# Attention block on one core: SyncE's wait for the output stores moved behind the closing barrier, its first loads moved ahead of the block

## Chip, cores, metric

One core of one Trainium2 chip. The metric is the device time of one execution in microseconds (us); each kernel is run several times, and where two kernels are compared they ran in turns on the same chip. A run more than 1.5% above the fastest of its kernel counts as slow. Names: PE is the matmul engine TensorE, DVE is VectorE, ACT is ScalarE, POOL is GpSimd, SP is SyncE. "L146" is line 146 of the kernel's file.

## The reference, cut to what matters

```python
B, Sq, D = 32, 4, 1024;  Hq, Hkv, Sk, Dh = 32, 4, 2048, 128      # all bf16
q = (x @ wq)                       # per head
p = softmax(q k^T * Dh**-0.5)      # over the cached keys; 8 query heads share one k/v head
out = (p v) @ wo
```

k_cache and v_cache are 64 MiB each, wq and wo 8 MiB each: some 151 million bytes (151 MB) have to be read once, and 0.26 MB are written.

## The kernel before

Each engine gets a list of operations with explicit semaphore waits. SyncE's list is nearly all loads; its first eight entries wait for nothing.

```python
p.dma("sp", ... x_sb <- x ..., [], "x", "s_x")
for c in range(4):
    p.dma("sp", ... w_sb[2c:2c+2] <- wq ..., [], ("wq", c), f"s_w{c}")
...                                  # then k(0), k(1), k(2) without waits, then v(0), k(3), ... with waits
# the end: two stores of half the columns each, one issued by SyncE, one by ScalarE
for j, (n0, n1, waits) in enumerate(((0, NA, (0,)), (NA, D, (1, 2)))):
    p.dma(("sp", "act")[j], ... out[:, n0:n1] <- y_sb[:, n0:n1] ..., [("oe", i) for i in waits], ("out", j), f"s_o{j}")
...
p.op("sp", lambda e: None, [("out", j) for j in range(2)])   # SyncE waits until both stores have landed

block = es.enter_context(nc.Block())
@block.gpsimd
def _(eng): p.emit("pool", eng, sems)
@block.sync
def _(eng): p.emit("sp", eng, sems)
...                                  # the same for tensor, vector, scalar
```

Two barriers of all engines surround this, and neither is written in the lines above. One belongs to the constructor of the program (its line in the kernel before is L534) and comes first. The other is what leaving the block emits (L146). Entering the block puts no barrier there: SyncE's wait in the constructor's barrier ends at 0.669 us and its first load starts at 0.737, with no record between them. (That a jump on each engine lies there is my reading of the program.) A barrier, as the records of L146 have it: every engine drains, SyncE last (360.962), and the four other than GpSimd count up one semaphore; GpSimd waits for these four (360.994) and counts up a second one (361.072), and each engine leaves when it sees that (361.131 to 361.178).

## Time and profile before

| | us |
|---|---|
| time, median of 6 runs (362.99 to 363.22) | 363.11 |
| span of the profile, first to last instruction | 361.18 |
| x load issued; first load packet | 0.74; 1.76 |
| end of the last load packet | 357.57 |
| last semaphore increments by the two stores ("landing") | 360.27 and 360.72 |
| SyncE's last record ends | 361.13 |

The time of the profiled run, 362.99, is 1.8 us longer than its span: the semaphore records go on after the kernel's last instruction, until 363.12. What they belong to is called the closing work below.

How busy the DMA was. From the table by stage, kernel before; the columns after the stretch are its length, the busy time of PE, weight loads, DVE, ACT and POOL, the granted clock, the DMA share and GB/s:

```profile
core 0: us, PE busy (x) PEld busy (x) DVE busy (x) ACT busy (x) POOL busy (x), PEclk, DMA share, GB/s
0.00:10.00 10.00, 2.50 (x12) 0.93 (x9) 0.69 (x1) 1.28 (x1) 8.83 (x11) 1.00 0.86 341
10.00:50.00 40.00, 35.14 (x169) 3.89 (x37) 20.89 (x21) 8.61 (x15) 6.83 (x16) 1.00 1.00 428
50.00:150.00 100.00, 89.76 (x915) 45.23 (x718) 90.43 (x52) 34.55 (x34) 52.83 (x87) 1.00 1.01 428
...
330.00:347.00 17.00, 15.23 (x225) 11.87 (x204) 8.47 (x13) 2.06 (x6) 3.12 (x3) 1.00 1.00 418
347.00:357.40 10.40, 9.32 (x64) 2.07 (x22) 0.00 (x0) 0.00 (x0) 0.00 (x0) 1.00 0.95 374
```

The DMA share is 1.00 or 1.01 in every stretch from 10 to 347 us and 0.95 in the last 10 us of loads, and in the packet records the load queue has no gap over 0.05 us from its first packet to 357.57: the body is bound by loads. A change at the two ends can save what lies before the first packet and after the last one, and nothing else.

The start, from the timeline of the kernel before (start, duration, engine, line, operation; "SPq" is SyncE's sequencer):

```profile
0.24 0.10 POOL L534 MEMSET const-float32-0.0<- 128x1 f32 x1 [0.24 <-issue]
...
0.73 0.20 POOL L231 MEMSET ident<- 128x128 bf16 x1 [0.29 <-POOLq L534]
0.73 1.28 ACT L281 ACT_TABLE_LOAD   x1 [0.73 <-PEq L534]
0.74 0.38 SPq L187 DMA_DIRECT2D P_sb<-in_x_dram  x1
1.17 1.85 SPq L190 DMA_DIRECT2D big<-in_wq_dram  x4
```

GpSimd, ScalarE and SyncE start at 0.73 to 0.74, behind the barrier of L534, from which SyncE, the first to drain (0.00), leaves at 0.67 (PE's first work waits until 3.7 for x, VectorE's for PE). That is the constructor's barrier; the block, which comes after, holds nobody up.

The end, from the instructions of L146, the block's closing barrier, in the kernel before ("xcount: duration ns min/median/max, first and last start us"):

```profile
L146 POOLq EVENT_SEMAPHORE  x2: 17/17/17, 361.0 to 361.1; - x2
...
L146 ACTq DRAIN  x1: 152/152/152, 359.4 to 359.4; - x1
L146 SPq COMPARE_BRANCH  x1: 33/33/33, 360.8 to 360.8; - x1
L146 SPq DRAIN  x1: 7/7/7, 361.0 to 361.0; - x1
L146 SPq EVENT_SEMAPHORE  x1: 17/17/17, 361.1 to 361.1; - x1
```

and from the waits of SyncE's queue in the same kernel (us in total, times, longest):

```profile
SPq L82 <- DMA out_dram<-P_sb: 1.8, 1, 1.8
SPq L534 <- PEq L534: 0.7, 1, 0.7
```

ScalarE has drained by 359.5. SyncE waits 1.8 us for the stores, and only then drains; the four others stand in the barrier until 361.1 because of it. So barrier and landing are in series.

### The profile page before, as it was taken

Reading aid. Unit: us, or ns where it says so; the run is one execution under the profiler, and the core shown is the slowest. Engines: PE = TensorE matmul, PEld = TensorE weight load, DVE = VectorE, ACT = ScalarE, POOL = GpSimd, SP = SyncE. Lnnn points to the kernel's source line nnn. Section 1 sums busy time; section 2 is a strip of 40 time slices with the busy share of each in tenths; the row PEclk is TensorE's granted clock in tenths of the full one; section 3 lists DMA queues with packets and bytes.
Section 4 is the critical chain, followed back from the end, with each engine's and each line's share of the span. In section 5 each row is a group of like instructions: output and inputs, shape, how many; then the busy total and the mean of one; then the engine's idle time right before and its main releaser. Section 6 shows DMA issues by size and latency. Waiting matters only on the chain. (4 is left out here: it accounts for less than half of the span.)

```text
span 361.2 us, 6248 instructions
## 1 busy us (share of the span) xinstructions
PE 307.2 (85%) x3030; PEld 147.0 (41%) x2340; DVE 269.4 (75%) x171; ACT 102.6 (28%) x110; POOL 165.4 (46%) x262
## 2 busy tenths in 40 slices
PE   1988788999999999988999888888888899889896
PEld 1002000454445544444444444444333444449721
DVE  0018799999899898879998888898888888866501
ACT  1014222333333333333333333323322233333000
POOL 8002055355555555554455444445555554444000
PEclk9999999999999999999999999999999999999999
DMA  8999999999999999999999999999999999999996
GB/s 323 432 435 434 419 428 430 434 418 425 431 426 430 423 430 432 429 423 430 430 428 425 431 428 430 423 432 428 432 423 430 430 430 423 430 430 430 411 416 225
DMA packets 12251, 151.66 MB, mean 420 GB/s; under 512 B 1360, under 2 KB 2128, under 8 KB 2768
## 3 DMA queue, kind: packets, MB, share of 16 engines
q1 hardware_dynamic: 12096, 151.39, 99.0%
q8 instruction: 6, 0.10, 0.1%
q10 hardware_dynamic: 144, 0.13, 0.1%
q14 instruction: 5, 0.04, 0.0%
HBM read 151.26 MB, written 0.26 MB: 420 GB/s over the span
## 5 line engine op out<-in xcount | busy, mean ns | idle before, releaser
L328 DVE STREAM_TRANSPOSE KT_sb<-big 128x2048 f32<-128x2048 f32 x64 | 146.6, 2293 | 16.6 <-DMA big<-in_k_cache_dram 16.6
L354 ACT ACTIVATE P_sb<-ps_s,negmx 128x2048 bf16<-128x2048 f32 x32 | 82.1, 2565 | 184.8 <-DVE negmx L350 184.8
L16 PE MATMUL ps_s<-KT_sb,QD_sb 128*128 128x512 bf16 x384 | 103.7, 377 | 0.0
L385 POOL COPY PD_sb<-PT_sb 32x1024 f32<-32x1024 f32 x62 | 64.1, 1034 | 63.4 <-PE ps_r L394 60.6
L385 POOL COPY big<-PT_sb 32x1024 f32<-32x1024 f32 x61 | 63.0, 1034 | 59.0 <-PE ps_r L394 56.2
L350 DVE TENSOR_REDUCE negmx<-ps_s 128x1 f32<-128x2048 f32 x32 | 73.2, 2286 | 12.4 <-PE ps_s L16 10.8
L394 PE MATMUL ps_r<-big 128*128 128x128 bf16 x1024 | 59.8, 219 | 11.5 <-PEq L85 11.5
L394 PE MATMUL ps_r<-big,PD_sb 128*128 128x128 bf16 x1024 | 59.8, 219 | 9.9 <-PEq L85 9.9
L394 PEld LDWEIGHTS ps_r<-big 128*128 128x128 bf16 x1024 | 57.9, 98 | 22.3 <-issue 21.8
L394 PEld LDWEIGHTS ps_r<-big,PD_sb 128*128 128x128 bf16 x1024 | 58.0, 98 | 21.1 <-issue 20.6
L341 PE MATMUL ps_s<-KT_sb,QD_sb 128*128 128x512 bf16 x128 | 48.3, 377 | 18.3 <-PEq L85 18.3
L341 PEld LDWEIGHTS ps_s<-KT_sb,QD_sb 128*128 128x128 bf16 x128 | 12.3, 96 | 102.9 <-issue 102.9
L363 DVE STREAM_TRANSPOSE PT_sb<-P_sb 128x1024 f32<-128x1024 f32 x32 | 39.8, 1245 | 15.8 <-ACT P_sb L354 15.8
L318 POOL COPY QD_sb<-QT_sb 32x64 f32<-32x64 f32 x128 | 29.4, 230 | 46.0 <-DVE QT_sb L297 20.3
L16 PE MATMUL ps_r<-ident 128*128 128x384 bf16 x173 | 33.3, 325 | 0.0
L366 PEld LDWEIGHTS ps_r<-ssum,permf 128*128 128x128 f32 x64 | 11.9, 187 | 24.8 <-issue 23.1
L403 ACT ACTIVATE QT_sb<-ps_r,rinv 128x128 bf16<-128x128 f32 x32 | 11.7, 367 | 29.7 <-PE ps_r L394 27.5
L279 DVE TENSOR_SCALAR KT_sb<-ps_r 128x512 bf16<-128x512 f32 x2 | 1.3, 686 | 19.8 <-PE ps_r L263 19.8
L16 PE MATMUL ps_s<-big,KT_sb 128*128 128x224 bf16 (+1 forms) x62 | 12.0, 272 | 1.2 <-DVE KT_sb L410 1.1
L420 PE MATMUL ps_s<-big,KT_sb 128*128 128x512 bf16 (+1 forms) x32 | 11.8, 375 | 1.0 <-DMA big<-in_wo_dram 1.0
L434 DVE CAST P_sb<-ps_s 128x512 bf16<-128x512 f32 (+1 forms) x2 | 1.1, 542 | 15.2 <-PE ps_s L420 15.2
L252 PE MATMUL ps_r<-ident 128*128 128x384 bf16 x32 | 10.3, 322 | 0.0
(41 smaller groups left out, 85.2 us busy)
## 6 DMA issues: line engine op xcount, KB each, us to landing
big<-in_k_cache_dram SPq DMA_DIRECT2D x32, 2048.0 KB, 18.6
big<-in_v_cache_dram SPq DMA_DIRECT2D x32, 2048.0 KB, 22.1
big<-in_wq_dram SPq DMA_DIRECT2D x4, 2048.0 KB, 13.9
big<-in_wo_dram SPq DMA_DIRECT2D x6, 1024.0 KB, 22.8
big<-in_wo_dram SPq DMA_DIRECT2D x2, 512.0 KB, 24.3
big<-in_wo_dram SPq DMA_DIRECT2D x2, 256.0 KB, 22.6
big<-in_wo_dram SPq DMA_DIRECT2D x4, 128.0 KB, 17.5
P_sb<-in_x_dram SPq DMA_DIRECT2D x1, 256.0 KB, 2.9
```

The source lines that it names most:

```text
L16: return eng.add_instruction(mybir.InstMatmult(name=nc.get_next_instruction_name(), engine=eng.engine, start_tensor_calc=start, stop_tenso ...
L318: p.op("pool", lambda e, s=src, d=dst: e.tensor_copy(d, s), waits if g == 0 else [("pt", i - 2)] * (g == 1 and i > 1), ("qd", i) if g == G ...
L328: p.op("dve", lambda e, s=src, d=dst: e.transpose(d, s), waits, ("kt", i, c), gives="t_kt" if c else None)
L341: mm = lambda e, a_=(out_, lhsT, rhs), f=first, l=last: e.matmul(a_[0], lhsT=a_[1], rhs=a_[2], start=f, stop=l, skip_group_check=True)
L350: p.op("dve", lambda e: e.tensor_reduce(negmx[:, i % 4:i % 4 + 1], ps_s[:, :], AX.X, ALU.max, negate=True), [("qk", i)], ("negmx", i))
L354: p.op("act", lambda e: e.activation(P_sb[:, :, :, :].rearrange("p t r w -> p t w r"), ps_s[:, :].rearrange("p (t w r) -> p t w r", w=2, r=R),
L363: p.op("dve", lambda e: e.transpose(dst, src), [("exp", i)], ("pt", i))
L366: p.op("pe", lambda e: e.matmul(ring[(i if i == L else i // 2 * 2) % 4][:, 510 + i % 2:511 + i % 2], lhsT=permf[:, :], rhs=ssum[:, i % 4:i ...
L385: p.op("dve" if i >= B - 2 and g < i - B + 4 else "pool", lambda e, s=src, d=dst: e.tensor_copy(d, s), [free] * (g == 0 or i >= B - 2) + [ ...
L394: p.op("pe", lambda e: e.matmul(buf[:, 0:Dh], lhsT=pd_of(i)[:, t // 2, :, :, :, t % 2].rearrange("p x g q -> p (x g q)"), rhs=big[:, slot_ ...
L403: p.op("act", lambda e: e.activation(dst, src, ACT.Copy, scale=rinv[:, i % 4:i % 4 + 1]), [("pv", i), ("rinv", i)], ("o", i))
L420: mm = lambda e, a=(out_, lhsT, rhs): e.matmul(a[0], lhsT=a[1], rhs=a[2], start=(u == 0), stop=(u == Hq - 1), skip_group_check=True)
```

## The change

Its intent: start the loads sooner, by taking them out of the block, and let the closing barrier run while the stores are still on their way. SyncE still ends only after both have landed.

```diff
-    def emit(self, name, engine, sems):
+    def emit(self, name, engine, sems, start=0, end=None):
...
-        ops = self.ops[name]
+        ops = self.ops[name][start:end]
...
-        p.op("sp", lambda e: None, [("out", j) for j in range(2)])
-        block = es.enter_context(nc.Block())
+        lead = next(n for n, o in enumerate(p.ops["sp"]) if o[1] or o[2])
+        p.emit("sp", nc.sync, sems, 0, lead)
+        with nc.Block() as block:
...                                   (sync now emits from `lead` on; the others as before)
+        for j in range(2):
+            s, n = p.at["out", j]
+            nc.sync.wait_ge(sems[s], n)
```

`lead` is 8: x, the four parts of wq and the first three k loads.

More of the change, by code (lines that the diff above doesn't have):

```diff
@@ L495, in bass_standalone__gqa_block_cached__sampling_kernel, with _ @@
         sems = {n: es.enter_context(nc.semaphore(f"e_{n}" if n in p.ENGINES else n)) for n in names}
-        p.op("sp", lambda e: None, [("out", j) for j in range(2)])
-        block = es.enter_context(nc.Block())
-        @block.gpsimd
-        def _(eng):
-            p.emit("pool", eng, sems)
-        @block.sync
-        def _(eng):
-            p.emit("sp", eng, sems)
-        @block.tensor
-        def _(eng):
-            p.emit("pe", eng, sems)
-        @block.vector
-        def _(eng):
-            p.emit("dve", eng, sems)
-        @block.scalar
-        def _(eng):
-            p.emit("act", eng, sems)
+        lead = next(n for n, o in enumerate(p.ops["sp"]) if o[1] or o[2])
+        p.emit("sp", nc.sync, sems, 0, lead)
+        with nc.Block() as block:
+            @block.gpsimd
+            def _(eng):
+                p.emit("pool", eng, sems)
+            @block.sync
+            def _(eng):
+                p.emit("sp", eng, sems, lead)
+            @block.tensor
+            def _(eng):
+                p.emit("pe", eng, sems)
+            @block.vector
+            def _(eng):
+                p.emit("dve", eng, sems)
+            @block.scalar
+            def _(eng):
+                p.emit("act", eng, sems)
+        for j in range(2):
+            s, n = p.at["out", j]
+            nc.sync.wait_ge(sems[s], n)
     return nc
```

## The prediction

> What bounds the kernel. The 40-slice view shows about 430 GB/s; the table by stage gives a DMA share of 1.00 to 1.01 from 10 to 347 us. In the packet records the load queue has no gap above 0.05 us from its first packet at 1.76 us to 357.6 us. So the body is bound by reading 151 MB, which the change doesn't touch; only the two ends can move.
>
> Start. The barrier that ends at 0.7 us (drain, then a semaphore wait on each engine) carries the line of the constructor of the program, not of the block. It stays ahead of the moved loads. Between SyncE's semaphore wait (0.65 to 0.67 us) and the x load (0.74) there are only 68 ns; its later issues have gaps of 42 to 55 ns. The block has no opening barrier, only a jump, and none is recorded there. [...] this trace leaves room for 13 to 26 ns. So moving the eight loads without waits (x, four wq, also three k) is worth 0 to 0.03 us.
>
> End. SyncE issues its store at 358.53, ScalarE at 358.95 to 359.33. The stores land (last semaphore increments) at 360.27 and 360.72. Then comes a serial tail: SyncE's wait record ends 360.76, a compare-and-branch until 360.83, its drain 360.96, GpSimd gathers at 360.99 and releases at 361.07, the engines leave at 361.13 to 361.18, the end of the span. That is 0.46 us after the last landing.
> [...] issue to landing is 1.7 to 1.8 us. The change doesn't shorten that; it puts the barrier inside it. ScalarE's drain ends at 359.52, so the barrier can close at about 359.7 (+0.17, as in the present tail), a microsecond before the landing. Afterwards the span ends with SyncE's last wait, about 360.72 + 0.03 = 360.76 (360.82 if the two waits come in the other order). Span: 361.18 - 0.42 = 360.76.
>
> After the span. The time is 1.8 us longer than the span: closing work that follows the kernel. In the semaphore records, its first round of increments by all engines takes 0.53 us, with one hop of 0.21 us, where the next round takes 0.36 with all engines waiting. I read it as an engine that left the barrier late. With four engines arriving a microsecond early, this hop should shrink: 0.17 us, perhaps more if SyncE stands late in that chain.
>
> Sum: 363.1 - 0.42 - 0.17 - 0.02 = 362.5 us. Range 362.15 to 362.85. 2% would be 7 us: not possible.
>
> What would show it right: first packet still near 1.76 us and x issued within 0.05 us of 0.74; SyncE's drain right after its store's issue, GpSimd's release near 359.6, and SyncE's waits last, ending at 0.03 to 0.1 us after the last landing. The time should fall by more than the span.
>
> What would make it wrong: the runtime's closing work waiting on something else, so that the span shrinks and the time doesn't; ScalarE's or SyncE's drain waiting for its own store (they took 0.15 and 0.01 us here); a chip whose load rate differs by 0.1%, which is as much as the whole effect.

(The sum comes to 363.1 - 0.42 - 0.17 - 0.02, about 362.5: the 0.42 is read from the present tail, the 0.17 is my estimate, and the 0.02 lies within the 13 to 26 ns, the 68 ns less the 42 to 55 ns of the later gaps. "By all engines" and "with all engines waiting" are my reading: the semaphore records don't say which engine counts.)

## The result and the profile after

The change took 362.15 us (median of 6 runs, 362.08 to 362.87) against 363.11 before. The ratio is 0.9978, with a 95% interval of 0.9965 to 0.9991. (A ratio here is the mean time of one kernel's fast runs over that of the other's of the same rounds, so it isn't quite the ratio of the medians.) Run again later, on chips 4 and 13, it gave 362.13 and 362.14, against 363.00 both times: a gain of 0.86 to 0.96 us, where 0.6 was predicted. That is a quarter of a per cent; that it is a gain is shown by three sets of runs whose intervals leave out 1, and where it comes from by the traces.

The start, from the timeline of the kernel after:

```profile
0.73 1.28 ACT L281 ACT_TABLE_LOAD   x1 [0.73 <-PEq L539]
0.73 0.20 POOL L231 MEMSET ident<- 128x128 bf16 x1 [0.29 <-POOLq L539]
0.74 0.38 SPq L187 DMA_DIRECT2D P_sb<-in_x_dram  x1
1.18 1.85 SPq L190 DMA_DIRECT2D big<-in_wq_dram  x4
```

Nothing moved: x is issued at 0.740 instead of 0.737, behind the same barrier (L539 is the constructor's line here). The first packet comes at 1.76 as before.

The end, from the instructions of the closing barrier (L499) and of the wait behind it (L523) in the kernel after:

```profile
L499 POOLq EVENT_SEMAPHORE  x2: 17/17/17, 359.6 to 359.6; - x2
...
L499 SPq DRAIN  x1: 124/124/124, 359.0 to 359.0; - x1
L499 ACTq DRAIN  x1: 152/152/152, 359.4 to 359.4; - x1
L499 SPq EVENT_SEMAPHORE  x1: 17/17/17, 359.7 to 359.7; - x1
```

```profile
L523 SPq EVENT_SEMAPHORE  x1: 28/28/28, 360.8 to 360.8; - x1
```

and from the waits of its SyncE queue:

```profile
SPq L523 <- DMA out_dram<-P_sb: 1.0, 1, 1.0
```

SyncE drains at 359.0 instead of 361.0, the barrier is over at 359.7 instead of 361.1, and what remains of SyncE's wait for the stores is 1.0 us instead of 1.8. The stores land where they did, at 360.74 (before: 360.72). The wait's record, one instruction for both stores, ends 0.045 us after that, and the span with it: 361.18 became 360.79.

That is 0.39 us. The time fell by more than twice as much, so over half of the gain lies after the span. What is there to read are the semaphore records. One of them, number 2, is named by no instruction of the kernel. In this trace it is counted up nine times in a round (each count is a "hop" below): in one round that ends at the kernel's first instruction (the trace holds an earlier one too), and in two rounds after the kernel. Most of the other semaphores have one more update between these two (234 semaphores in the kernel after, from 361.03 to 361.64 us), the first of them during the last hops of the first round; I take these for resets. The round before the kernel takes 0.37 us in both traces and the second round after it 0.355 and 0.356, which I take for a round that no late engine holds up. In us from the landing of the last store:

| | SyncE's last record ends | hop 1 | hop 4 | hop 5 | hop 9 | last hop of round 2 |
|---|---|---|---|---|---|---|
| before | 0.409 | 0.695 | 0.984 | 1.007 | 1.225 | 2.400 |
| after | 0.045 | -0.749 | -0.461 | 0.167 | 0.331 | 1.475 |

Before, the whole first round came after the landing. After, four of its nine hops are over before the stores have landed, hop 5 waits for SyncE (it comes 0.122 us after SyncE's last record; the experiments below test this), and four more follow. The first round, hop 1 to hop 9, takes 1.080 us instead of 0.530, as it now holds that wait. The sum of it: -0.364 until SyncE's last record, -0.476 from there to hop 5, -0.054 from hop 5 to hop 9, -0.031 after that, and the landing itself 0.022 later: -0.903. The -0.031 is the pause between the rounds, which is scatter: it is 0.820 us before, 0.788 after, and 0.788 again with the start half alone, whose end is as before. In 12 of the 14 traces the measured time is the last hop's time (from the first instruction) less 0.125 to 0.136 us, so these hops are indeed what the time ends with. The two others are told below.

### The profile page after: what moved, and what is told of

Read it like the earlier page. It is cut to its first block, busy times and chain, and to the rows that moved or that the text cites. A ratio compares the mean times of both kernels' runs of the same rounds, so it can differ in the third digit from the quotient of the medians.

```text
span 360.8 us, 6251 instructions
## 1 busy us (share of the span) xinstructions
PE 307.6 (85%) x3034; PEld 147.0 (41%) x2340; DVE 269.5 (75%) x171; ACT 102.8 (28%) x110; POOL 165.9 (46%) x262
```

## The experiments

Theory: the whole gain is at the end; it is that the closing barrier and the first four hops now lie under the flight of the stores. Rivals: the earlier loads carry part; or the barrier got cheaper; or the closing work just starts when the last engine is there; or it is the form of the wait that gains.

Scatter: single runs of nearly every kernel, that before too, lie 0.3 to 1.7 us above the others, with the excess in the span and at a clock of 0.995 to 1.000; one run of before was slow (812.1) and is left out of the ratios. "Time minus span" below is less disturbed by that.

### The change again

No edit; it is the yardstick of the first set.

> The change as it is, again, as the yardstick of this set. Both theories: 362.1 to 362.2 us (median of its six runs 362.15), about 0.95 below the kernel before; span 360.8. One of its six runs was 362.87: if about one run in six is 0.5 us or more above the others again, the change carries a scatter of its own; if not, that run was chance.

Measured: 362.13 (362.07 to 362.49), before 363.00, ratio 0.998 (0.9967 to 0.9994); span 360.8; time minus span 1.27 to 1.33 (1.8 in the kernel before). None of these five runs is half a microsecond above its median, nor of the six of the later set, while the kernel before has such runs too (364.65); so the 362.87 is no sign of a scatter that the change brings.

### Each half alone

Start half: SyncE's two waits put back inside the block.

```diff
+        p.op("sp", lambda e: None, [("out", j) for j in range(2)])
         lead = next(...)
...
-        for j in range(2):
-            s, n = p.at["out", j]
-            nc.sync.wait_ge(sems[s], n)
```

> Only the start half: the eight loads ahead of the block, SyncE's waits for the stores inside the block as before. Theory (all of the gain is at the end): within 0.05 us of the kernel before, 363.1; x issued at 0.74 us, tail with the drain of SyncE after the stores' landing. Rival (the earlier loads carry part of it): 0.1 to 0.5 us faster than before, x issued earlier than 0.70 us.

Measured: 363.07 (363.04 to 363.20) against 363.00; ratio 1.0002 (0.9989 to 1.0015). x is issued at 0.737, hop 9 comes 1.225 us after the landing, both exactly as before. (The interval of the ratio is 0.13% or 0.47 us to each side, too wide to exclude the rival's 0.1 to 0.5 us; the issue time does.)

End half:

```diff
-        lead = next(n for n, o in enumerate(p.ops["sp"]) if o[1] or o[2])
-        p.emit("sp", nc.sync, sems, 0, lead)
+        lead = 0
```

> Only the end half: SyncE waits for the stores after the closing barrier, all loads inside the block. Theory: the same as the change itself, 362.15, within 0.1 us; SyncE's drain at 358.95, its last wait at 360.76. Rival (the start carries part): slower than the change by what the start half gained, 0.1 to 0.5 us.

Measured: 362.21 (five runs 362.08 to 362.26, one 363.87 whose excess is all in the span); ratio 0.9987 (0.9972 to 1.0001), which reaches 1 because that run is counted. Hop 9 comes 0.330 us after the landing, as with the whole change. So the end half is the change, and the start half gains nothing; the first rival falls.

### Loads ahead of the barrier that does hold them up

If the loads bound the body from the first packet on, the start half failed only because it moved them past the wrong thing. Here they go between SyncE's drain of the constructor's barrier and its wait for that barrier's release. The drain stays in front, so the other engines are not kept waiting by eight issues.

```diff
+        main = nc.m.functions[0].blocks[0]
+        order = list(main.instructions)
+        drain = next(n for n, o in enumerate(order) if type(o).__name__ == "InstDrain" and o.engine == mybir.EngineType.SP)
+        loads_first = [o for o in order if type(o).__name__ == "InstDMACopy"]
+        rest = [o for o in order if type(o).__name__ != "InstDMACopy"]
+        main.instructions = rest[:drain + 1] + loads_first + rest[drain + 1:]
```

> The change, with the eight loads moved once more: between SyncE's first drain and its wait of the opening barrier of the program, so that no barrier at all stands ahead of them. Theory (loads bound the body from the first packet on, and the change did not move them because that barrier stayed ahead): x issued at 0.05 to 0.1 us instead of 0.74, first packet near 1.1 instead of 1.76, and the whole stream, span and time earlier by 0.6 to 0.65 us than the change: 361.5. Rival (the start is not on the critical path, as something other than loads sets the first stage, or slack later swallows it): x is as early, the time stays at 362.1.

Measured: 361.46 (361.38 to 361.57), correct; ratio to before 0.9956 (0.9943 to 0.997). That is 0.67 us below the change in the same rounds and 1.54 below the kernel before: the fastest version. From its timeline:

```profile
0.08 0.38 SPq L187 DMA_DIRECT2D P_sb<-in_x_dram  x1
...
0.52 1.89 SPq L190 DMA_DIRECT2D big<-in_wq_dram  x4
0.73 1.28 ACT L281 ACT_TABLE_LOAD   x1 [0.73 <-PEq L547]
```

and from the instructions of the constructor's line there:

```profile
L547 SPq DRAIN  x1: 7/7/7, 0.0 to 0.0; - x1
...
L547 ACTq EVENT_SEMAPHORE  x1: 17/17/17, 0.7 to 0.7; - x1
...
L547 SPq EVENT_SEMAPHORE  x1: 17/17/17, 4.0 to 4.0; - x1
```

x goes out at 0.08 instead of 0.74, while ScalarE still leaves the barrier at 0.7 and SyncE, with its eight issues done, at 4.0. First packet 1.10 instead of 1.76; the last load packet ends at 357.02 instead of 357.58. The DMA stream came forward by 0.66 us at its start and, in the profiled run, by 0.56 at its end (this run, 361.57, is the slowest of the five); by the medians nothing downstream swallowed it.

### A barrier's price where nothing hides it

The kernel before, with one more barrier behind the closing one.

```diff
+        nc.all_engine_barrier()       # behind the block; SyncE's waits inside the block
```

> The kernel before with one more all-engine barrier behind the block's closing one; SyncE waits for the stores inside the block, as before. It prices one barrier where nothing hides it: in the trace a drain, gather and release take about 0.2 us from the engines' leaving one barrier to leaving the next, so 363.0 + 0.2 = 363.2 (0.15 to 0.35 more than before). Both theories expect that.

Measured: 363.47 (363.33 to 364.07) against 363.02. The median is 0.45 us higher, more than the 0.15 to 0.35 expected, and the fastest runs differ by 0.37. In the trace SyncE's last records in the two barriers start at 361.90 and 362.23: one barrier takes 0.33 us, at the upper edge of what I had expected. Hop 9 comes 0.32 us later after the landing than in the kernel before.

### The same in the change: one and four more barriers

```diff
+        for _ in range(1):            # and 4
+            nc.all_engine_barrier()
         for j in range(2):
             s, n = p.at["out", j]
             nc.sync.wait_ge(sems[s], n)
```

> The change with one more all-engine barrier between the closing one and SyncE's waits. Theory (the barrier and the first half of the closing chain lie under the landing of the stores, with 0.6 us to spare between the fourth hop at 360.28 and the fifth at 360.9): no change in time, 362.13 within 0.1; fourth hop later by one barrier, fifth in place. Rival (part of the gain is that the barrier itself got shorter, and its cost is still on the path): slower than the change by the price of a barrier, 0.2 us or more.

Measured: 362.29 (362.07 to 362.47) against 363.02, on another chip than the first set. The median is 0.16 us above the change's 362.13, a little outside the 0.1 that I had allowed, and the excess is not at the end: in the profiled run the last load packet ends 0.33 us later than in the change. Time minus span is 1.27 to 1.33, that of the change. Hop 4 came 0.136 us before the landing (0.461 in the change: later by one barrier), hop 5 at 0.167 and hop 9 at 0.331, unmoved. The barrier that cost 0.33 in the kernel before costs nothing after the landing here.

> The change with four more barriers. Theory: 4 barriers at 0.2 to 0.25 us push the fourth hop to 361.1 to 361.3, past the 360.9 where SyncE's own hop came; only the excess shows, about 4u - 0.6, so 0.2 to 0.4 us slower than the change: 362.3 to 362.5. Rival (no hiding): 4u = 0.8 to 1.0 us slower, 363.0 or more.

Measured: 363.42 (363.30 to 364.78): 1.28 us slower than the change, where I had expected 0.2 to 0.4, and just what the rival's four barriers at 0.33 would make. By the total alone the rival would win. The hops say otherwise: hop 9 comes 1.090 after the landing, 0.76 later than in the change, which is four barriers (1.32) less some 0.6. The rest, 0.45, falls into the second round: its second-to-third hop takes 0.122 instead of 0.038 and its fifth-to-sixth 0.47 instead of 0.10. There the packet records have one instruction fetch of 8 KB, at 362.81 for 0.38 us, that neither the kernel before nor the change has, and the long fifth-to-sixth hop spans most of it (362.84 to 363.32). So my number was low because a barrier costs 0.33 and not 0.2 to 0.25, and by 0.45 us in the second round, which has nothing to do with hiding; that the fetch caused it is likely by its time, but no run shows it. Because two chips were involved, the ladder was run again.

### The ladder on one chip: 0, 2 and 3

> The change again, on the chip of this set, as the foot of a ladder of 0, 2 and 3 extra barriers: the earlier ladder compared two chips. Both theories: 362.1 to 362.2; fifth hop of the closing chain 0.62 us behind the fourth.

> The change with two more barriers, each 0.33 us in the traces of the runs with one and four (taken in place of the 0.2 to 0.25 that I had assumed). Theory: 0.66 us is just the room of 0.6 us, so 0.05 to 0.1 us slower than the change. Rival (barriers are not hidden): 0.66 us slower.

> The change with three more barriers. Theory: 0.99 - 0.6 = 0.35 to 0.45 us slower than the change; if its program, as that with four, draws one more instruction block in the closing work (a packet near 362.8 us), 0.45 more on top, visible in the second round of hops and not in the first. Rival: 1.0 us slower, with the first round of hops later by that.

| extra barriers | time, median | hop 4 | hop 5 | hop 9 | last hop of round 2 |
|---|---|---|---|---|---|
| 0 | 362.14 | -0.460 | 0.167 | 0.331 | 1.476 |
| 1 (other chip) | 362.29 | -0.136 | 0.167 | 0.331 | 1.502 |
| 2 | 362.49 | 0.191 | 0.215 | 0.433 | 1.580 |
| 3 | 363.19 | 0.540 | 0.564 | 0.782 | 1.929 |
| 4 (other chip) | 363.42 | 0.848 | 0.872 | 1.090 | 2.687 |

Hops in us from the landing. Hop 4 moves by a third of a microsecond with each barrier. Hop 5 doesn't move at all for the first, by 0.05 for the second, and in step with hop 4 from there on; hop 9 by 0, 0.10, 0.45 and 0.76. That is the theory's curve, not the rival's straight line.

The times with two and three barriers are higher than the hops explain, and by the totals alone three barriers would again speak for the rival, who expected 1.0. With three barriers the time is 1.05 us above the change; the hops hold 0.45 of it, and the second round, where I had looked for the rest, takes 0.358 us as ever. An instruction fetch starts at 363.12, after the last hop, and in this profiled run the time is 0.64 us past the last hop instead of 0.13 before it; its six runs fall into two at 362.7 and four at 363.1 to 363.4. With two barriers the time is 0.35 above the change, where I had expected 0.05 to 0.1 and the rival 0.66; the hops hold 0.10. In the profiled run 0.21 of the rest comes after the last hop (the time is 0.08 past it), where this trace has no record and no fetch. These are the two exceptions announced above. What those 0.21 us are stays open; that it is the same sort of fetch is only a guess.

### ScalarE waits in SyncE's place

```diff
-            nc.sync.wait_ge(sems[s], n)
+            nc.scalar.wait_ge(sems[s], n)
```

> The change with ScalarE, not SyncE, waiting for the stores behind the barrier. Theory (the closing work passes from engine to engine in a fixed order, four hops come before SyncE's, and four after, so SyncE is the place where a late engine costs least): a late ScalarE holds up more hops, 0.1 to 0.5 us slower than the change, 362.2 to 362.6; fewer than four hops before the stores have landed. Rival (the order doesn't matter, the closing work just starts when the last engine is there): same as the change, 362.13 within 0.05.

Measured: 362.42 (362.33 to 362.76) against 363.02. The one record of the wait is now ScalarE's:

```profile
L523 ACTq EVENT_SEMAPHORE  x1: 38/38/38, 360.8 to 360.8; - x1
```

Only hop 1 came before the landing (-0.744); hop 2 at 0.173, hop 9 at 0.496 instead of 0.331. Time minus span (ScalarE's wait ends the span now) 1.43 to 1.52 instead of about 1.3. So the hops have an order: ScalarE's wait leaves one hop before the landing and SyncE's four (hop 4 at -0.461 in the change), so that ScalarE is the second and SyncE the fifth, and the one that waits holds up all hops behind its own. That SyncE is where a late engine costs least stays my theory: of the five engines only these two were tried. The rival of no order falls.

### The kernel before without its closing barrier

The wait stays where it was, in the block; the barrier's instructions are taken out. Results are still right, as both stores wait for everything that the other engines compute, and SyncE waits for the stores.

```diff
+        end = nc.m.functions[0].blocks[-1]       # the 11 instructions of the closing barrier
+        end.instructions = []
```

> The kernel before with the closing barrier removed and SyncE's waits left inside the block; correct, as SyncE's stores wait for all that the others computed. Theory (what counts is that no barrier follows the wait, not where the wait stands): like the change, 362.15, at most 0.17 slower, as its last wait rides on the jump out of the block, which took 0.16 us to the next instruction; four hops of the closing chain long before the landing. Rival (the move of the wait itself, or the waits in one instruction, is what gains): 362.5 or more.

Measured: 362.31 (362.24 to 362.36) against 363.00 before and 362.14 for the change. Hops 1 to 4 were over a microsecond before the landing; hop 5 at 0.316, that is 0.149 later than in the change, and the time is 0.17 higher. SyncE's last record is no longer a plain wait but the compare-and-branch out of the block, which carries the second wait and had 0.16 us from its start to the next instruction in the kernel before too. So the place of the wait matters only in that no barrier comes after it; the last rival falls, except for these 0.15 us, for which the trace leaves only the form of the wait.

## Why the prediction was right or wrong

- What bounds the kernel: right. DMA share 1.00 to 1.01 from 10 to 347 us before and after, and moving the stream forward by 0.66 us at its start (x issued at 0.08 instead of 0.74) brought 0.67 us.
- Start, "worth 0 to 0.03 us": right. x at 0.740 instead of 0.737; the half alone 363.07 against 363.00. The barrier ahead of the loads is the constructor's, not the block's.
- End of the span: right. 361.18 - 0.42 = 360.76 was predicted, 360.79 measured; the barrier over at 359.7; the waits last, 0.045 us after the landing. SyncE's drain took 0.12 us rather than 0.01, without consequence.
- "After the span ... this hop should shrink: 0.17 us, perhaps more if SyncE stands late in that chain": the direction was right, the size was not, nor was the reason for it. This is the mis-sized term. From the end of the span to hop 9 took 0.769 us before and 0.286 after, 0.48 less, and 0.51 less to the last hop. I counted the excess of one long hop (0.21 us, between hop 2 and hop 3). That hop is no shorter after the change: it is 0.210 again. All engines still leave one barrier shortly before (361.13 to 361.18 with hop 2 at 361.45 before the change, 359.71 to 359.76 with hop 2 at 360.03 after it); with ScalarE waiting, where hop 3 comes long after that, and in the run without a closing barrier it is 0.038. What the change takes off is not the length of that hop but everything up to and including hop 4, because SyncE, the one engine that waits, is the fifth of nine; of this the prediction had only its "perhaps more". The ScalarE run shows what the place is worth: three hops fewer come before the landing, and hop 9 comes 0.165 us later.
- The sum: 362.5 predicted, 362.15 measured, on the lower edge of the range of 362.15 to 362.85. The range held because it had been left wide, not because the sum was near.

## What to carry to other kernels

In this kernel it paid to put the wait for the last stores behind the barrier and the drains that can run while they fly (0.86 to 0.96 us), and on the engine with the later place in the closing work (SyncE rather than ScalarE, hop 9 at 0.331 against 0.496; the other three were not tried): try both elsewhere. Here the flight of 1.77 us, from the issue of the last store to its landing, hides one barrier more than the kernel has (hop 9 at 0.331 with and without it). Before moving instructions ahead of a barrier, look up whose barrier the trace shows them waiting for: taking the loads out of the block passed no barrier and gave nothing, moving them past the constructor's gave 0.67 us. Read the gain after the profile's span too: over half of this one is there.
